# GpSimd's elementwise steps cut into pieces of about 128 columns, in a fused attention, FFT and feed-forward kernel

## The chip, the cores and the metric

The kernel runs on one core of a Trainium2 chip. The metric is the time of one execution on the device in microseconds (us), the median of the runs; less is better.

## What is computed

Inputs are q, k, v of 8 batches x 8 heads x 576 positions x 64, and two weight matrices. All are float32, but the weights, which come as 64-bit floats.

```python
def _attn_ref(q, k, v):
    scores = scale * np.matmul(q, k.transpose(0, 1, 3, 2))
    mask = (rel >= 0) & (rel < 64)
    ...
    return np.matmul(attn, v).astype(np.float32)

def _moe_ref(x, w_ch1, w_ch2):
    X = np.fft.fft(np.fft.fft(x, axis=1), axis=2)
    u = x + np.real(X).astype(np.float32)
    un = (u - mean(u)) / np.sqrt(var(u) + 1e-06)
    return u + np.maximum(un @ w_ch1, 0.0) @ w_ch2
```

So it is attention in a window of 64 positions, a two-dimensional FFT of its result (576 positions by 512 features) of which the real part is added, a normalisation and a feed-forward layer of 512 to 2048 to 512.

## The kernel before

The 8 x 576 = 4608 rows are cut into 36 tiles T of 128 rows; each pair of batches has 9 tiles. The work has four kinds of stages.

`attn_tile(T)` computes attention for a tile. From tile 13 on (`PRO`) operands are split into two float16 parts, a high one (a cast, on ACT or DVE) and a low one, the difference between the float32 value and the high part. The low part is one elementwise subtraction on POOL or DVE: `k_lo` (line 484, 512 columns, from `kn`), `q_part(1)` (line 495, 1024 columns, from `qn`) and `p_lo` (line 620, 512 columns, from `pr`, twice a tile). The parts lie in the buffer `flex` and are turned by transposing DMAs that SP sends: `kst` (line 487), `qbd` (line 499) and `pt` (line 626). TensorE (PE) then computes scores `psc` (line 575) and the product `pa` (line 657). VectorE (DVE) applies the mask (line 587) and scales to `xu` (line 669). `radix4` (line 691) makes five sums `y` of the tile's columns: four instructions, the first two of 256 columns, the last two of 128. The high and low part `yp` of `y` (lines 405 and 758) are turned too, and `keep` (line 718) adds the turned parts into `yT`.

`fft(b)` folds `yT` and makes sums of 388 columns (lines 804 to 858), which PE multiplies by constant matrices (`pg`, `pz`, lines 890 and 924). The result goes to DRAM (`md`).

`norm_tile(T)` gathers rows of `md` (line 998, a DMA that POOL issues), adds them to `xu`, takes mean and variance, the reciprocal root `rs` on POOL (line 1022) and the scaled `un` on DVE (line 1026). Its low part `up` is `u_lo` (line 1045, 512 columns, on POOL or DVE), and a DMA turns it to `uhl`.

`ffn(c)` multiplies two tiles at a time by the weights: `ph` (line 1207), the parts `hh` (ACT, line 1222, and DVE, line 1225), `po` (line 1188), and the last sum into `xu` (line 1245). Its matmuls fill PE wherever the other stages leave room.

The order is made by `Plan.order()` while the program is built. Each step is an `op` with an engine, a duration in us, a priority and often a second engine (`alt`); the planner walks through time with these durations and fixes the engine of each step and the order on each engine. It takes POOL and the DVE steps that are marked `port` to exclude each other. The chip then runs each engine's list in that order, with semaphores between the engines. A step's function is called with the engine that was chosen (`eng`), and issues its instructions there.

Of the kernel before, what the change touches and what calls it, by code (L numbers as in the profile page):

```python
# [19 lines left out]
ALU = mybir.AluOpType  # L20
# [277 lines left out]
def attn_fft_ffn_kernel(ctx: ExitStack, tc: tile.TileContext, q, k, v, w1, w2, gidx, dft_d, dft_s, mask, out):  # L298
    nc = tc.nc
# [14 lines left out]
    op = plan.op  # L314
# [86 lines left out]
    def copy(eng, out, in_, scale=None):  # L401
# [4 lines left out]
        else:  # L406
            eng.tensor_copy(out, in_)

    xts, Bx, yTs, ByT, ByL, uhls, Bu, mds, Bmd = ({} for _ in range(9))

    def attn_tile(T, base):
        pb, n = divmod(T, NT)
# [4 lines left out]
        t = {}  # L417
# [39 lines left out]
        if whole:  # L457
            bpk, bpq = Buf("ps"), Buf("ps")

            def flip(dst, src):  # L460
                t[dst] = bank("ps", f"{dst}{T}")
                for hp in range(4):
                    heads = t[src][:, 2 * hp : 2 * hp + 2].rearrange("p h d -> p (h d)")
                    nc.tensor.transpose(t[dst][:, hp], heads, ident)

            def q_copy(h, eng):
                src = t["pq"][64 * h : 64 * h + 64].rearrange("p a (j s) -> p a j s", j=2)
                copy(eng, qbd32[i][64 * h : 64 * h + 64, :, :, h, :], src)

            op("PE", 0.44, base, lambda: flip("pk", "kn"), [bk, Bid], [bpk, bkT])  # L470
            op("ACT", 0.48, base + 0.1, lambda e: copy(e, kst_, t["pk"]), [bpk], [bkT], alt=("DVE", 0.6), port=False)
            op("PE", 0.44, base + 0.5, lambda: flip("pq", "qn"), [bq, Bid], [bpq, Bq[i]])
            for h in range(2):
                op("ACT", 0.48, base + 0.6, lambda e, h=h: q_copy(h, e), [bpq], [Bq[i]], alt=("DVE", 0.6), port=False)
        else:
            bkp = Bfl[0]

            def k_hi(eng):
                t["kp"] = half[:, 0].rearrange("p (h z d) -> p h z d", h=H, z=2)
                copy(eng, t["kp"][:, :, 0], t["kn"])  # L480

            def k_lo(eng):
                kp = t["kp"]
                eng.tensor_tensor(out=kp[:, :, 1], in0=t["kn"], in1=kp[:, :, 0], op=ALU.subtract)  # L484

            def k_turn():
                nc.sync.dma_start_transpose(kst_, t["kp"].rearrange("p h z d -> p (h z d)"))

            def q_part(z, eng):
                hi, lo = qpad[:, :, 0::3], qpad[:, :, 1:3]  # L490
                src = t["qn"][:, :, None, :].to_broadcast([P, H, 2, D])
                if z == 0:
                    copy(eng, hi, src)
                else:
                    eng.tensor_tensor(out=lo, in0=src, in1=hi, op=ALU.subtract)  # L495

            def q_turn(j):
                src = qpad[64 * j : 64 * j + 64].rearrange("p h x d -> p (h x d)")
                nc.sync.dma_start_transpose(qbd[i][:, j].rearrange("p h (z s) -> p (h z) s", z=2), src)  # L499

            op("ACT", 0.52, base, k_hi, [bk], [bkp], alt=("DVE", 0.34, lazy))
            op("POOL", 1.12, base + 0.1, k_lo, [bk], [bkp], alt=("DVE", 0.6, lazy))
            op("DMA", TURN, base + 0.2, k_turn, [bkp], [bkT], lat=2.0)
            op("ACT", 0.95, base + 0.5, lambda e: q_part(0, e), [bq], Bfl[4:6], alt=("DVE", 0.6, lazy))
            op("POOL", 2.1, base + 0.6, lambda e: q_part(1, e), [bq], Bfl[4:6], alt=("DVE", 1.13, lazy))
            for j in range(2):
                op("DMA", TURN, base + 0.7, lambda j=j: q_turn(j), Bfl[4:6], [Bq[i]], lat=2.8)
# [49 lines left out]
        for jj in range(2):  # L557
            J = 2 * n + jj
            m = ((192 if jj else 128) if J % 9 == 0 else (64 if jj else 0))
# [57 lines left out]

            def p_lo(eng, jj=jj):
                pp = t["pp", jj]
                eng.tensor_tensor(out=pp[:, :, 1], in0=t["pr", jj], in1=pp[:, :, 0], op=ALU.subtract)  # L620

            def p_turn(h, jj=jj):
                if h == 0:
# [58 lines left out]
        def radix4(eng):  # L682
            y = t["y"] = sb([P, 5, P], F32, "y", f"y{T}")
            x4 = xts[T].rearrange("p (a e) -> p a e", a=4)
            for o, p0, p1, al in (
                (y[:, 0::4], x4[:, 0:2], x4[:, 2:4], ALU.add),
                (y[:, 2:4], x4[:, 0:2], x4[:, 2:4], ALU.subtract),
                (y[:, 1], y[:, 0], y[:, 4], ALU.subtract),
                (y[:, 0], y[:, 0], y[:, 4], ALU.add),
            ):  # L690
                eng.tensor_tensor(out=o, in0=p0, in1=p1, op=al)  # L691

        op("POOL", 2.35, base + 7, radix4, [bx], [by], alt=("DVE", 1.2, LAZY_Y if T < 4 else lazy))
        first, keeps = [], []
        for bb in range(2):
# [11 lines left out]
            def keep(eng, bb=bb, b=b, lo=lo, hi=hi):  # L707
                if n == 0 and not soon:
                    yTs[b] = sb([P, 4, S + 1], F32, "yT", f"yT{b}")
                spans = [(lo - S * bb, lo - P * n, hi - lo)]  # L710
                if n == 0:
                    spans.append((S, 0, 1))
                for d_, o, m in spans:
                    dst, src = yTs[b][:, :, d_ : d_ + m], t["py"][..., o : o + m]
                    if soon:
                        copy(eng, dst, src, YS)
                    else:
                        eng.tensor_tensor(out=dst, in0=src[:, 0], in1=src[:, 1], op=ALU.add)

            if lo == S * bb and n > 0:  # L720

# [67 lines left out]
    def fft(b, base):  # L789
        pb, bb = divmod(b, 2)  # L790
        lazy = LAZY_FFT if b else plan.MARGIN
        t = {}
# [5 lines left out]
        def fold(which, c0, c1, eng):  # L798
            yT = yTs[b]
            fw, bw = yT[:, :, c0:c1], yT[:, :, S - c0 : S - c1 : -1]  # L800
            if which == 0:
                if "xe" not in t:
                    t["xe"], t["xo"] = sb([P, 4, HS + 1], F32, "xe", f"xe{b}"), yT[:, :, 0 : HS + 1]
                eng.tensor_tensor(out=t["xe"][:, :, c0:c1], in0=fw, in1=bw, op=ALU.add)
            else:
                eng.tensor_tensor(out=fw, in0=fw, in1=bw, op=ALU.subtract)

        if bb == 0:
            low.append((ByL[b], Buf()))
# [8 lines left out]
        for x, (nm, src, bsrc, o_sum, o_dif) in enumerate((("f", "xe", 1, 0, 2), ("h", "xo", 0, 2, 0))):  # L818
# [3 lines left out]
            def view(src):  # L822
                s_ = t[src]
                return s_[:, :, 0:NJ], s_[:, :, 192 : 192 + NJ], s_[:, :, 192 : 192 - NJ : -1]


            def first(eng, which, al, nm=nm, src=src):
                a0, up, dn = view(src)
                t[nm, which] = sb([P, 4, NJ], F32, "r3", f"{nm}{which}_{b}")
                eng.tensor_tensor(out=t[nm, which], in0=up, in1=dn, op=al)  # L830

            def mid(nm=nm, src=src):
                t[nm, 1] = sb([P, 4, NJ], F32, "r3", f"{nm}1_{b}")
# [2 lines left out]
                )  # L836

            def tot(eng, nm=nm, src=src):
                eng.tensor_tensor(out=t[nm, 0], in0=t[nm, 0], in1=view(src)[0], op=ALU.add)

            pr = base + 1 + x
            two = {"alt": ("POOL", 0.95, lazy)}
# [4 lines left out]
            for r in (2, 1, 0):  # L847
# [7 lines left out]

                def rest(eng, r=r, nm=nm):
                    s_ = t[nm, r, "v"]
                    eng.tensor_tensor(out=s_[:, 1], in0=t[nm, r], in1=s_[:, 0], op=ALU.subtract)

                op("ACT", 0.42, pr + 0.1, part, [b3[r]], [bfh[nm, r]], alt=("DVE", 0.27))  # L860
                op("DVE", 0.47, pr + 0.2, rest, [b3[r]], [bfh[nm, r]], **two)
# [124 lines left out]
    def norm_tile(T, base):  # L986
# [55 lines left out]
            copy(eng, t["up"][:, 0], t["un"])  # L1042

        def u_lo(eng):
            eng.tensor_tensor(out=t["up"][:, 1], in0=t["un"], in1=t["up"][:, 0], op=ALU.subtract)  # L1045

        def u_turn():
            new_u()
# [269 lines left out]
```

## Time and profile before

| | us |
|---|---|
| median of 3 runs | 1019.76 |
| the runs | 1015.79, 1019.76, 1021.48 |
| the profiled execution, first to last instruction | 1015.3 |
| PE busy in it | 972.7 (96%) |
| DVE busy | 679.6 (67%) |
| ACT busy | 417.9 (41%) |
| POOL busy | 197.4 (19%), 203 instructions |

The profiled execution is one of its own; its span, 1015.3 us, is all of its time that the profile shows. [...] An engine's busy time counts an instruction from its start to its end, waits for a shared resource within it too. In brackets behind a row of the timeline stands how long the engine was idle before it and what ended that.

### The profile page before, as it was taken

Reading aid. Unit: us, or ns where it says so; the run is one execution under the profiler, and the core shown is the slowest. Engines: PE = TensorE matmul, PEld = TensorE weight load, DVE = VectorE, ACT = ScalarE, POOL = GpSimd, SP = SyncE. Lnnn points to the kernel's source line nnn. Section 1 sums busy time; section 2 is a strip of 40 time slices with the busy share of each in tenths; the row PEclk is TensorE's granted clock in tenths of the full one; section 3 lists DMA queues with packets and bytes.
Section 4 is the critical chain, followed back from the end, with each engine's and each line's share of the span. In section 5 each row is a group of like instructions: output and inputs, shape, how many; then the busy total and the mean of one; then the engine's idle time right before and its main releaser. Section 6 shows DMA issues by size and latency. Waiting matters only on the chain.

```text
span 1015.3 us, 22449 instructions
## 1 busy us (share of the span) xinstructions
PE 972.7 (96%) x8756; PEld 687.3 (68%) x8756; DVE 679.6 (67%) x1979; ACT 417.9 (41%) x1047; POOL 197.4 (19%) x203
## 2 busy tenths in 40 slices
PE   8889989999999989998999999999999999999998
PEld 7677757676676657665676666766676667676665
DVE  5899899888777767565787769676686636441121
ACT  6666656744554335323354335333453213121111
POOL 1000100042244223332022302233021300220000
PEclk9999999999999999999999999999999999999999
DMA  8987673235989866878668766867565421230000
GB/s 194 244 224 198 191 188 109 71 78 94 160 152 178 160 114 143 142 137 141 126 111 172 144 126 108 173 131 161 89 111 108 94 38 37 60 74 21 1 22 21
DMA packets 310538, 123.06 MB, mean 121 GB/s; under 512 B 292568, under 2 KB 292696, under 8 KB 310432
## 3 DMA queue, kind: packets, MB, share of 16 engines
q1 hardware_dynamic: 307712, 112.71, 54.8%
q0 software_dynamic: 2720, 8.92, 3.3%
q8 instruction: 69, 1.13, 0.5%
q14 instruction: 37, 0.30, 0.1%
HBM read 54.97 MB, written 14.17 MB: 68 GB/s over the span
## 4 chain that ended last, share of the span: by engine, by line
PE 75%; DVE 8%; DMA 8%; SPq 5%; ACT 2%; issue 2%; POOL 0%; DVEq 0%; ACTq 0%; POOLq 0%
PE ph L1207 30%; PE po L1188 30%; PE pz L924 3%; PE pa L657 3%; DMA pt<-flex 2%; DMA kn<-in_k 2%; PE pg L890 2%; PE psc L568 2%; PE psc L575 2%; SPq L626 2%; SPq L499 1%; DVE y L691 1%; PE pp L606 1%; SPq L427 1%; DVE pr L587 1%
## 5 line engine op out<-in xcount | busy, mean ns | idle before, releaser
L1207 PE MATMUL ph<-uhl,w0s 128*128 128x256 f16 (+1 forms) x3384 | 427.1, 277 | 10.1 <-DVE hh L1225 10.1
L1188 PE MATMUL po<-w1s,hh 128*128 128x512 f16 (+1 forms) x1696 | 428.1, 389 | 0.0
L1207 PEld LDWEIGHTS <-w0s 128*128 128x128 f16 x3264 | 318.0, 98 | 97.6 <-issue 14.5
L1225 DVE SCALAR_TENSOR_TENSOR hh<-ph,hh 128x256 f16<-128x256 f32 x272 | 114.5, 422 | 231.7 <-ACT hh L1222 225.8
L1222 ACT ACTIVATE hh<-ph 128x256 f16<-128x256 f32 x272 | 103.6, 382 | 392.9 <-PE ph L1207 297.1
L1188 PEld LDWEIGHTS <-hh 128*128 128x128 f16 x1632 | 157.0, 98 | 138.8 <-issue 1.9
L595 ACT ACTIVATE pr<-pr,nm 128x128 f32<-128x128 f32 x288 | 90.9, 392 | 13.2 <-DVE nm L587 13.1
L587 DVE CUSTOM_DVE_ANT_0 pr<-psc,mskb 128x128 f32<-128x128 f32 x288 | 65.5, 285 | 15.3 <-PE psc L568 11.3
L1045 POOL TENSOR_TENSOR up<-un,up 128x512 f16<-128x512 f32 x33 | 39.7, 1204 | 75.8 <-ACT up L403 73.1
L620 POOL TENSOR_TENSOR flex<-pr,flex 128x512 f16<-128x512 f32 x23 | 27.4, 1190 | 133.8 <-ACT flex L403 93.5
L1022 POOL TENSOR_TENSOR rs<-mv,mhalf 128x1 f32<-128x1 f32 x36 | 21.0, 584 | 157.9 <-DVE mv L1018 152.2
L484 POOL TENSOR_TENSOR flex<-kn,flex 128x512 f16<-128x512 f32 x19 | 25.0, 1314 | 125.0 <-ACT flex L403 119.3
L998 POOL DMA_INDIRECT mt<-md,gix x34 | 36.5, 1073 | 57.4 <-DMA md<-mp 48.8
L657 PE MATMUL pa<-va,pt 128*64 128x65 f16 (+1 forms) x760 | 39.3, 205 | 7.5 <-DMA pt<-flex 7.5
L657 PE MATMUL pa<-ve,pt 128*64 128x65 f16 (+1 forms) x760 | 39.4, 205 | 0.3 <-DMA ve<-va 0.3
L403 ACT CAST flex<-pr 128x512 f16<-128x512 f32 x39 | 24.0, 615 | 23.5 <-DMA pt<-flex 21.1
L691 DVE TENSOR_TENSOR y<-xu 128x256 f32<-128x256 f32 x68 | 32.1, 512 | 0.6
L669 DVE TENSOR_TENSOR xu<-pa,rc 128x256 f32<-128x256 f32 x72 | 30.6, 425 | 2.6
L568 PE MATMUL psc<-kst,qbd 128*128 128x128 f32 x208 | 28.2, 282 | 3.1 <-ACT qbd L403 1.2
L924 PE MATMUL pz<-g,ds__75 97*96 97x257 f16 (+3 forms) x240 | 29.3, 273 | 1.4 <-DVE g L900 1.4
L657 PEld LDWEIGHTS <-pt 128*64 128x64 f16 x1104 | 20.7, 113 | 14.7 <-DMA pt<-flex 7.9
L495 POOL TENSOR_TENSOR flex<-qn,flex 128x1024 f16<-128x1024 f32 x12 | 26.2, 2187 | 16.3 <-ACT flex L403 14.1
(155 smaller groups left out, 1108.0 us busy)
## 6 DMA issues: line engine op xcount, KB each, us to landing
wd<-in_moe_w_ch SPq DMA_DIRECT2D x20, 512.0 KB
out<-xu SPq DMA_DIRECT2D x36, 256.0 KB
ve<-va SPq DMA_DIRECT2D x67, 130.0 KB
kn<-in_k SPq DMA_DIRECT2D x32, 256.0 KB
qn<-in_q SPq DMA_DIRECT2D x32, 256.0 KB
flex<-in_moe_w_ch SPq DMA_DIRECT2D x12, 512.0 KB
flex<-in_v SPq DMA_DIRECT2D x20, 256.0 KB
md<-mp SPq DMA_DIRECT2D x24, 192.0 KB
```

The lines of the kernel that those rows point to most:

```text
L568: nc.tensor.matmul(p_[:, hp], qw, keys(hp, jj), start=True, stop=True)
L587: nc.vector.tensor_tensor_reduce(out=t["pr", jj][:, hp], in0=t["ps", jj][:, hp], in1=mskb[:, m : m + P], scale=-0.125, scalar=3.0e38, op0= ...
L595: nc.scalar.activation(pr, pr, AF.Exp, bias=t["nm", jj][:, hp : hp + 1], scale=-1.0)
L657: nc.tensor.matmul(pa[64 * jj : 64 * jj + 64, hh], pt[:, sl], v_, start=(x == 0), stop=(x == len(mm) - 1))
L691: eng.tensor_tensor(out=o, in0=p0, in1=p1, op=al)
L924: nc.tensor.matmul(pz[:M, c0:c1], ds_[:NJ, a, c[0] : c[0] + c[1]], t["g", gi][:, b_, c0:c1], start=(x == 0), stop=(x == len(mm) - 1),)
L998: nc.gpsimd.indirect_dma_start(out=mts[T], out_offset=None, in_=mds[pb][0 : HR if n < 4 else 2 * HR], in_offset=bass.IndirectOffsetOnAxis( ...
L1045: eng.tensor_tensor(out=t["up"][:, 1], in0=t["un"], in1=t["up"][:, 0], op=ALU.subtract)
L1188: nc.tensor.matmul(t["po"][i], l_, r_, start=(f == 0 and x == 0), stop=(f == NKF - 1 and x == len(mm) - 1))
L1207: nc.tensor.matmul(ph, l_, r_, start=(x == 0), stop=(x == len(mm) - 1))
L1222: nc.scalar.activation(t["hh", f][:, 0], ph, AF.Relu)
L1225: nc.vector.scalar_tensor_tensor(out=hh[:, 1], in0=ph, scalar=0.0, in1=hh[:, 0], op0=ALU.max, op1=ALU.subtract)
```

## The change

A helper `both` takes the place of single elementwise instructions with two inputs. If the engine is POOL it cuts the step along the second dimension into `n` pieces, each an instruction of its own; on DVE it stays one instruction. The planner's durations and priorities are the same, and so are the order on all engines and the choice of the engine for each step.

```diff
+    def both(eng, out, in0, in1, al, n=4):
+        w = out.shape[1] // n if eng is nc.gpsimd else out.shape[1]
+        for k in range(0, out.shape[1], w):
+            eng.tensor_tensor(out=out[:, k : k + w], in0=in0[:, k : k + w], in1=in1[:, k : k + w], op=al)
...
             def k_lo(eng):
                 kp = t["kp"]
-                eng.tensor_tensor(out=kp[:, :, 1], in0=t["kn"], in1=kp[:, :, 0], op=ALU.subtract)
+                both(eng, kp[:, :, 1], t["kn"], kp[:, :, 0], ALU.subtract)
...
                 else:
-                    eng.tensor_tensor(out=lo, in0=src, in1=hi, op=ALU.subtract)
+                    both(eng, lo, src, hi, ALU.subtract, 8)
...
             def p_lo(eng, jj=jj):
                 pp = t["pp", jj]
-                eng.tensor_tensor(out=pp[:, :, 1], in0=t["pr", jj], in1=pp[:, :, 0], op=ALU.subtract)
+                both(eng, pp[:, :, 1], t["pr", jj], pp[:, :, 0], ALU.subtract)
...
-                (y[:, 1], y[:, 0], y[:, 4], ALU.subtract),
-                (y[:, 0], y[:, 0], y[:, 4], ALU.add),
+                (y[:, 1:2], y[:, 0:1], y[:, 4:5], ALU.subtract),
+                (y[:, 0:1], y[:, 0:1], y[:, 4:5], ALU.add),
             ):
-                eng.tensor_tensor(out=o, in0=p0, in1=p1, op=al)
+                both(eng, o, p0, p1, al, o.shape[1])
...
-                        eng.tensor_tensor(out=dst, in0=src[:, 0], in1=src[:, 1], op=ALU.add)
+                        both(eng, dst, src[:, 0], src[:, 1], ALU.add, 4 if m > 1 else 1)
...
         def u_lo(eng):
-            eng.tensor_tensor(out=t["up"][:, 1], in0=t["un"], in1=t["up"][:, 0], op=ALU.subtract)
+            both(eng, t["up"][:, 1], t["un"], t["up"][:, 0], ALU.subtract)
```

The same edit is made in the FFT's folds and sums (lines 804 to 858), of which POOL has two steps of 388 columns, cut in four.

On POOL, where the normalisation of tiles 6 to 8 meets the first split queries (`qn`), the list of instructions before was:

```order
L998 DMA mt_2773<-md_993,gix 128x512
L1045 TENSOR_TENSOR up_2796<-un_2793,up_2796 128x512
L495 TENSOR_TENSOR flex<-qn_1913,flex 128x8x128
L1022 TENSOR_TENSOR rs_2902<-mv_2880,mhalf 128x1
L998 DMA mt_2914<-md_993,gix 128x512
```

On POOL in the same place it is with the change (line numbers are 6 higher, and the helper's line 413 stands for each cut step):

```order
L1004 DMA mt_2788<-md_993,gix 128x512
L413 TENSOR_TENSOR up_2811<-un_2808,up_2811 128x128 x4
L413 TENSOR_TENSOR flex<-qn_1919,flex 128x128 x8
L1028 TENSOR_TENSOR rs_2927<-mv_2905,mhalf 128x1
L1004 DMA mt_2939<-md_993,gix 128x512
```

Nothing has moved: a step is four or eight instructions in its old place, and the same holds along POOL's whole list. On PE, DVE, ACT and SP the lists are alike but for line numbers.

## Rows read from the trace of the kernel before

**Rows 1.** The page: busy time by engine (us, share, instructions), and the chain that ended last.

```profile
PE 972.7 (96%) x8756; PEld 687.3 (68%) x8756; DVE 679.6 (67%) x1979; ACT 417.9 (41%) x1047; POOL 197.4 (19%) x203
...
PE 75%; DVE 8%; DMA 8%; SPq 5%; ACT 2%; issue 2%; POOL 0%; DVEq 0%; ACTq 0%; POOLq 0%
```

**Rows 2.** Timeline of PE: start and duration (us), instruction [idle before, releaser].

```profile
229.44 0.66 PE L750 MATMUL py<-ident,y 128*128 128x128 f32 x4 [1.08 <-DVE y L691]
...
247.70 1.34 PE L575 MATMUL psc<-kst,qbd 128*64 128x128 f16 x32
...
270.33 0.63 PE L750 MATMUL py<-ident,y 128*128 128x128 f32 x4 [0.83 <-DVE y L691]
...
365.85 0.26 PE L657 MATMUL pa<-va,pt 128*64 128x65 f16 x1 [3.76 <-DMA pt<-flex]
...
442.17 0.60 PE L1207 MATMUL ph<-uhl,w0s 128*128 128x256 f16 x4 [0.74 <-DVE hh L1225]
...
466.76 0.49 PE L1207 MATMUL ph<-uhl,w0s 128*128 128x256 f16 x3 [2.79 <-DVE hh L1225]
```

**Rows 3.** Timeline of DVE, delayed and undisturbed steps; x2 are two instructions in a row.

```profile
225.22 1.71 DVE L691 TENSOR_TENSOR y<-xu 128x256 f32<-128x256 f32 x2
226.85 2.53 DVE L691 TENSOR_TENSOR y<-y 128x128 f32<-128x128 f32 x2
...
267.23 2.42 DVE L691 TENSOR_TENSOR y<-xu 128x256 f32<-128x256 f32 x2
269.58 0.60 DVE L691 TENSOR_TENSOR y<-y 128x128 f32<-128x128 f32 x2
...
347.22 2.50 DVE L758 SCALAR_TENSOR_TENSOR yp<-y,yp 128x512 f16<-128x512 f32 x1
...
438.31 2.16 DVE L758 SCALAR_TENSOR_TENSOR yp<-y,yp 128x512 f16<-128x512 f32 x1
...
459.22 2.10 DVE L620 TENSOR_TENSOR flex<-pr,flex 128x512 f16<-128x512 f32 x1 [0.67 <-ACT flex L403]
...
464.74 1.11 DVE L691 TENSOR_TENSOR y<-xu 128x256 f32<-128x256 f32 x2
...
772.45 0.76 DVE L691 TENSOR_TENSOR y<-xu 128x256 f32<-128x256 f32 x2
...
775.34 0.68 DVE L758 SCALAR_TENSOR_TENSOR yp<-y,yp 128x512 f16<-128x512 f32 x1
```

**Rows 4.** Timeline of POOL in three stretches.

```profile
225.44 1.21 POOL L1045 TENSOR_TENSOR up<-un,up 128x512 f16<-128x512 f32 x1 [0.62 <-ACT up L403]
226.61 2.30 POOL L495 TENSOR_TENSOR flex<-qn,flex 128x1024 f16<-128x1024 f32 x1
...
346.77 2.40 POOL L495 TENSOR_TENSOR flex<-qn,flex 128x1024 f16<-128x1024 f32 x1 [2.20 <-ACT flex L403]
...
454.77 1.15 POOL L1045 TENSOR_TENSOR up<-un,up 128x512 f16<-128x512 f32 x1 [6.92 <-ACT up L403]
455.88 0.56 POOL L1022 TENSOR_TENSOR rs<-mv,mhalf 128x1 f32<-128x1 f32 x1
```

**Rows 5.** POOL's instructions by form: count, busy us, mean ns of one, idle before, releasers.

```profile
L1045 POOL TENSOR_TENSOR up<-un,up 128x512 f16<-128x512 f32 x33 | 39.7, 1204 | 75.8 <-ACT up L403 73.1 <-issue 1.9 <-DVE up L407 0.8
...
L620 POOL TENSOR_TENSOR flex<-pr,flex 128x512 f16<-128x512 f32 x23 | 27.4, 1190 | 133.8 <-ACT flex L403 93.5 <-DVE flex L407 33.0 <-DMA kn<-in_k 6.1
L495 POOL TENSOR_TENSOR flex<-qn,flex 128x1024 f16<-128x1024 f32 x12 | 26.2, 2187 | 16.3 <-ACT flex L403 14.1 <-DVE flex L407 2.2
L484 POOL TENSOR_TENSOR flex<-kn,flex 128x512 f16<-128x512 f32 x19 | 25.0, 1314 | 125.0 <-ACT flex L403 119.3 <-DVE flex L407 5.5
...
L691 POOL TENSOR_TENSOR y<-y 128x128 f32<-128x128 f32 x4 | 1.8, 454 | 0.2
```

**Rows 6.** Timeline of SP's queue: first and last of eight rows in a stretch.

```profile
349.75 1.25 SPq L765 DMA_TRANSPOSE py<-yp  x1
...
361.25 1.32 SPq L626 DMA_TRANSPOSE pt<-flex  x1
```

More of the change, by code (lines that the diff above doesn't have):

```diff
@@ L803, in fold @@
                     t["xe"], t["xo"] = sb([P, 4, HS + 1], F32, "xe", f"xe{b}"), yT[:, :, 0 : HS + 1]
-                eng.tensor_tensor(out=t["xe"][:, :, c0:c1], in0=fw, in1=bw, op=ALU.add)
+                both(eng, t["xe"][:, :, c0:c1], fw, bw, ALU.add)
             else:
-                eng.tensor_tensor(out=fw, in0=fw, in1=bw, op=ALU.subtract)
+                both(eng, fw, fw, bw, ALU.subtract)
         if bb == 0:
@@ L829, in first @@
                 t[nm, which] = sb([P, 4, NJ], F32, "r3", f"{nm}{which}_{b}")
-                eng.tensor_tensor(out=t[nm, which], in0=up, in1=dn, op=al)
+                both(eng, t[nm, which], up, dn, al)
             def mid(nm=nm, src=src):
@@ L838, in tot @@
             def tot(eng, nm=nm, src=src):
-                eng.tensor_tensor(out=t[nm, 0], in0=t[nm, 0], in1=view(src)[0], op=ALU.add)
+                both(eng, t[nm, 0], t[nm, 0], view(src)[0], ALU.add)
             pr = base + 1 + x
@@ L857, in rest @@
                     s_ = t[nm, r, "v"]
-                    eng.tensor_tensor(out=s_[:, 1], in0=t[nm, r], in1=s_[:, 0], op=ALU.subtract)
+                    both(eng, s_[:, 1], t[nm, r], s_[:, 0], ALU.subtract)
                 op("ACT", 0.42, pr + 0.1, part, [b3[r]], [bfh[nm, r]], alt=("DVE", 0.27))
```

## The prediction

> **What bounds the kernel now.** I read the page first [rows 1]: TensorE (PE) is busy for 972.7 of 1015.3 us, and the chain of work that ended last spends 75% of its time on PE, 8% on VectorE (DVE), 8% on DMAs, 5% on SyncE's queue and 0% on GpSimd (POOL). So a change on POOL can only pay through a place where PE idles, and only if POOL stands behind that idle time by way of another engine. The reader is to see two things in these rows: that PE's idle time is only some 40 us in all, and that POOL, with 197.4 us of work, is far from being a limit itself.
>
> Then the timeline of PE, to find where it idles for what [rows 2]. After the first 200 us the long gaps are few. Five of them end with a DVE step or with a transposing DMA: 1.08 us at 229.44 (waits for `y`), 0.83 at 270.33 (`y`), 3.76 at 365.85 (`pt`), 0.74 at 442.17 and 2.79 at 466.76 (`hh`).
>
> Then the timeline of DVE just ahead of these gaps [rows 3], read against durations of the same step where nothing is beside it: the pair `y<-y` takes 0.60 us, the pair `y<-xu` 0.76, the step `yp` 0.68. At 226.85 the pair took 2.53, at 267.23 the pair `y<-xu` took 2.42, at 347.22 `yp` took 2.50, at 438.31 2.16. Beside the first and the third, POOL's timeline [rows 4] has a 1024-column step: 226.61 to 228.91, and 346.77 to 349.17. DVE's step ends about 0.5 us behind POOL's. So a DVE step that reads two operands from SBUF stands still while POOL reads SBUF, and goes on when POOL's instruction is over. The five gaps together are 9.2 us, which is about the whole stake: what else DVE loses beside POOL is time that PE never waits for.
>
> What happens when two POOL instructions stand back to back is in the same rows: `up` ends at 226.65 and the 1024-column step begins at 226.61, and yet the second `y<-xu` was over at 225.22 + 1.71 = 226.93, in the middle of the 1024-column step. DVE came in at the seam, for one instruction, and the next `y` then waited for the whole following POOL step. The two engines take turns, instruction by instruction. This is what the change acts on.
>
> **The change, part by part.** PE, DVE, ACT and SP keep their rows; nothing is moved past anything. On POOL, 75 steps of 512 columns become four pieces and 12 steps of 1024 columns become eight [rows 5], which is 75 x 3 + 12 x 7 = 309 more instructions; the five `yT` steps, two steps of 388 columns and two radix steps bring it to 334. The later pieces wait for nothing but older POOL work.
>
> Price of a piece. From 512 to 1024 columns POOL needs 2187 - 1204 = 983 ns more, 1.92 ns a column; so 1204 - 983 = 221 ns are fixed. A piece of 128 columns is then 246 + 221 = 467 ns, and the only step of 128 columns in the trace has 454 [rows 5]. A step of 512 columns goes from 1.20 to about 1.82 us (+0.62), one of 1024 from 2.19 to 3.63 (+1.45), and POOL has about 334 x 0.21 = 70 us more to do, some 267 us in 1015. As instructions overlap a little at the seams (0.04 us at 226.6), 0.17 a piece is the low end; 0.23 the high one. [...]
>
> What covers these 0.6 to 1.45 us. The first 1024-column step ends at 228.91, its transposes are sent right behind, and PE reads the result at 247.70 [rows 2, 4]: 19 us, against a step that ends 1.45 us later, or 3 us later with DVE's turns in between. That is the typical case for keys, queries and probabilities. The `up` steps feed a feed-forward chunk, which PE takes up only when it has nothing else to do. With that cover gone, each would cost its 0.6 to 1.45 us in full. One thing is queued on POOL with no cover: at 455.88 the reciprocal root `rs` starts the moment the `up` step from 454.77 is over [rows 4], and DVE waits for `rs`; it would come 0.6 us later. I count that in the last term below.
>
> The sum, place by place; after the change a DVE step waits for at most one piece, 0.45 us, each time it reads two operands:
> - 229.44: four `y` steps took 4.2 us (225.22 to 229.4) where they need 0.76 + 0.60 = 1.4 undisturbed. With three waits of a piece it is 2.7, so 1.5 less, more than the gap: -1.1.
> - 270.33: 2.42 - 0.76 = 1.66 us of waits, all in the first pair; the four `y` can now wait four times 0.45 = 1.8 while POOL goes on in pieces. Between 0 and -0.8; I take -0.2, as the waits nearly cancel.
> - 365.85: `yp` at 347.22 waited 2.50 - 0.68 = 1.82, now 0.45, so its transpose leaves 1.37 earlier than 349.75. From there SP sends eight rows without a real pause up to the `pt` transpose at 361.25 [rows 6] on which this gap ends. Against that, what came ahead of `yp` on POOL is 0.6 later. Between 0 and -1.4; I take -0.7, the middle.
> - 442.17: `yp` at 438.31 waited 1.48, the gap is 0.74: -0.7 (between 0 and -0.74).
> - 466.76: the step at 459.22 took 2.10 and needs about 0.69 (estimated as one 512-column step with two operands, like `yp`), so it gains 0.96; the four `y` at 464.74 waited 1.11 - 0.76 = 0.35 for a key step and may now wait up to 1.4. Between +0.5 and -1.8; I take -0.5.
> - All other places: shorter gaps ahead of which a DVE step waited (some 2 us of gap), against `rs` that is 0.6 later and new turns with `y`. I take 0, with -2 and +3 as ends.
>
> Together -3.2 us against the profiled execution's 1015.3 us, so 1012.1 us of span. That execution lies by the lowest of the three runs, 1015.79, and 4.5 below their median of 1019.76. The same 3.2 off the median gives **1016.6 us**. A measurement of this kernel can tell about 0.5%, 5.1 us, from no change, so this forecast counts as no difference. Its own range is 1013.5 to 1019.5.
>
> **The rivals.**
> 1. The waits go altogether, and PE gets all of it: 1.1 + 0.8 + 1.4 + 0.7 + 1.8 = 5.8 us, and 2 more from the short gaps, so 1012 to 1014. For it: all five gaps have a POOL step in their history, and one turn of DVE at the seam shows. Against it: a run of four `y` steps meets four pieces, where now it meets one step.
> 2. It becomes slower, by the turns. While POOL has a piece left, every two-operand DVE step waits for one. A run of four such steps beside a 512-column step waits up to 4 x 0.45 = 1.8, where it waited up to 1.2 once: 0.6 more, on some 80 steps, so 48 us more on DVE. As the chain has DVE on it for 8% of the span while DVE is busy for 67% [rows 1], about one eighth reaches the end: +6 us, 1025.8. It decides from the point where DVE's runs of two-operand steps beside POOL are on average longer than two. Against it: of the six delayed rows in [rows 3] three are single steps (347.22, 438.31, 459.22), and only `y` comes in runs.
> 3. The pieces don't let DVE in. Then a DVE step waits 0.6 to 1.45 longer in each of the five places, 3 to 6 us together with what lies between, 1023 to 1026. [...] The row at 225.22, where DVE came in at a seam of two overlapping steps, speaks against it.
> 4. It reaches nothing: DVE gets shorter, and PE's gaps stay since other transfers end there just as late. 1019 to 1021. For it: the 3.76 us gap ends with a DMA, and the rows between are SP's.
>
> **How the numbers follow.** Forecast 0.47, rival 1 0.22, rival 2 0.12, rival 3 0.05, rival 4 0.14. Rival 1 is mostly faster by over 0.5% (below 1014.7), as is a small part of the forecast's range: 0.25. Rival 2 and part of rival 3 are slower by over 0.5% (above 1024.9): 0.14. The rest, 0.61, is within. The range leaves out most of rival 2 and the far end of rival 1: 1011.5 to 1023.5.
>
> **What would show it.** POOL's busy time at 255 to 270 us and the pieces at 0.42 to 0.47 us each; the two `yp` steps at 1.2 or less and the 1024-column waits of over 1.5 us gone from DVE; DVE's busy time, 679.6 now, 3 to 15 us lower; the gaps of the first and the fourth place gone, and the third at 2.3 to 3.4. Wrong it would be if DVE's busy time rose, if new gaps of PE ended with `y` or `hh` behind runs of two-operand steps, or if POOL showed on the chain of waits.

## The result, and the profile after

The changed kernel takes 1010.51 us (median of 10 runs, 1003.20 to 1014.95) where the kernel before takes 1019.94 (10 runs, 1015.79 to 1023.75): a ratio of 0.9906, 95% interval 0.9877 to 0.9936. A second comparison later gave 0.9903 (0.9878 to 0.9927). So it is some 9.5 us faster. The prediction was 1016.6, with 1011.5 to 1023.5 as its range: right in sign, too small by a factor of three, and just outside the range.

The profiled execution of the changed kernel took 1003.44 us, 7 us below the median of its runs. A run's time is 1.7 to 1.9 us more than its span here, so that of before (span 1015.3) took some 1017, about 3 below its median. The two traces are therefore 13.8 us apart where the medians are 9.4 apart: they show more than a typical pair of runs would. The page of the changed kernel, busy time and chain, against [rows 1]:

```profile
span 1001.5 us, 22810 instructions
PE 967.4 (97%) x8756; PEld 685.3 (68%) x8756; DVE 665.6 (66%) x1979; ACT 418.2 (42%) x1047; POOL 260.9 (26%) x537
PE 80%; DMA 8%; SPq 3%; DVE 3%; issue 2%; ACT 2%; POOL 1%; DVEq 0%; POOLq 0%; ACTq 0%
```

The first thing to see is that PE's idle time, span less busy time, went from 42.6 to 34.1 us, and that PE's busy time went down as well, by 5.3 us with the same 8756 matmuls. DVE's share of the chain fell from 8% to 3%. POOL's busy time rose by 63.5 us, as the pieces cost what was forecast. POOL by form, against [rows 5] (count, busy us, mean ns of one, idle before it with the releasers):

```profile
L413 POOL TENSOR_TENSOR up<-un,up 128x128 f16<-128x128 f32 x132 | 56.0, 452 | 64.8 <-ACT up L403 62.2 <-issue 1.6 <-DVE up L407 0.8
L413 POOL TENSOR_TENSOR flex<-qn,flex 128x128 f16<-128x128 f32 x96 | 44.5, 496 | 14.1 <-ACT flex L403 10.9 <-DVE flex L407 3.2
```

PE's timeline, the gaps that answer to [rows 2] and one that is new:

```profile
309.09 0.22 PE L663 MATMUL pa<-va,pt 128*64 128x65 f16 x1 [2.10 <-DMA pt<-flex]
...
362.30 0.22 PE L663 MATMUL pa<-va,pt 128*64 128x65 f16 x1 [1.43 <-DMA pt<-flex]
...
459.29 1.47 PE L1213 MATMUL ph<-uhl,w0s 128*128 128x256 f16 x12 [1.30 <-DVE hh L1231]
```

The 3.76 us gap at `pt` is down to 1.43, the 2.79 at `hh` to 1.30; those of 1.08 (`y`), 0.83 (`y`) and 0.74 (`hh`) are gone. The 2.10 us at 309.09 are new. So is a gap that ends with `y`, one of the signs of being wrong that the prediction named; it is small:

```profile
367.26 0.63 PE L756 MATMUL py<-ident,y 128*128 128x128 f32 x4 [0.82 <-DVE y L413]
```

DVE's and POOL's timelines ahead of the `pt` gap show why; they answer to the row at 347.22 of [rows 3] and 346.77 of [rows 4]:

```profile
341.88 0.94 DVE L413 TENSOR_TENSOR y<-y 128x128 f32<-128x128 f32 x2
...
343.50 0.93 DVE L536 SCALAR_TENSOR_TENSOR va<-flex,va 128x512 f16<-128x512 f32 x1 [0.35 <-ACT va L534]
...
345.58 0.64 DVE L405 TENSOR_SCALAR yp<-y 128x512 f16<-128x512 f32 x1 [0.81 <-DVE hh L1231]
346.25 0.80 DVE L764 SCALAR_TENSOR_TENSOR yp<-y,yp 128x512 f16<-128x512 f32 x1
```
```profile
345.51 3.75 POOL L413 TENSOR_TENSOR flex<-qn,flex 128x128 f16<-128x128 f32 x8 [1.63 <-ACT flex L403]
```

`yp` takes 0.80 us where it took 2.50 and is over at 347.05, while the POOL step beside it goes on until 349.26. DVE comes in between pieces.

The fall of PE's busy time is in part the clock. Stretches behind the two long gaps, of the kernel before and then of the changed one (length; busy time of PE, its weight loads, DVE, ACT and POOL; the granted TensorE clock as a share; DMA share; GB/s):

```profile
365.00:370.00 5.00, 4.15 (x55) 2.71 (x56) 4.33 (x12) 1.25 (x2) 3.18 (x2) 0.66 0.33 53
...
460.00:470.00 10.00, 7.21 (x40) 4.19 (x40) 8.42 (x33) 4.93 (x13) 3.13 (x3) 0.89 1.00 153
470.00:480.00 10.00, 10.00 (x68) 6.66 (x67) 3.60 (x7) 2.08 (x4) 0.49 (x1) 0.94 0.76 153
```
```profile
365.00:370.00 5.00, 4.18 (x43) 2.96 (x42) 4.93 (x16) 2.14 (x6) 1.64 (x4) 1.00 0.70 121
...
460.00:470.00 10.00, 10.00 (x70) 6.66 (x69) 4.46 (x8) 2.46 (x5) 0.12 (x1) 1.00 1.01 202
470.00:480.00 10.00, 10.00 (x137) 6.90 (x136) 4.94 (x21) 3.85 (x10) 1.78 (x5) 1.00 0.48 74
```

Behind a gap of 3.76 us PE runs part of the next 5 us at a granted clock of 0.50 (366 to 368 of before): a mean of 0.66, so 5 x 0.34 = 1.7 us of work lost. Behind the gap of 2.79 us it is 10 x 0.11 + 10 x 0.06 = 1.7 again. In this trace of the changed kernel both stretches stand at 1.00. So 3.4 of the 5.3 us are clock that did not fall in these two places; the other 1.9 are not traced. My sum had no such term. It is not a sure gain: in a second trace of the changed kernel (`again`) both places stand at 1.00 too, but the clock fell behind the new gap at 309, which was 1.95 us long there, and the mean over the whole span was 0.993, as in before (0.996 in the first trace). The stretch behind that gap, from `again` and then from the first trace, where the gap was 2.10:

```profile
310.00:313.00 3.00, 3.00 (x33) 2.25 (x30) 1.40 (x6) 0.73 (x2) 2.08 (x5) 0.50 1.29 262
```
```profile
310.00:313.00 3.00, 3.00 (x23) 2.12 (x22) 2.28 (x8) 1.28 (x3) 1.44 (x4) 1.00 1.26 286
```

### The profile page after: what moved, and what is told of

Same layout as the page of the kernel before. It is cut to its first block, busy times and chain, and to the rows that moved or that the text cites. A ratio compares the mean times of both kernels' runs of the same rounds, so it can differ in the third digit from the quotient of the medians.

```text
span 1001.5 us, 22810 instructions
## 1 busy us (share of the span) xinstructions
PE 967.4 (97%) x8756; PEld 685.3 (68%) x8756; DVE 665.6 (66%) x1979; ACT 418.2 (42%) x1047; POOL 260.9 (26%) x537
## 3 DMA queue, kind: packets, MB, share of 16 engines
q8 instruction: 69, 1.13, 0.5%
## 4 chain that ended last, share of the span: by engine, by line
PE 80%; DMA 8%; SPq 3%; DVE 3%; issue 2%; ACT 2%; POOL 1%; DVEq 0%; POOLq 0%; ACTq 0%
PE ph L1213 34%; PE po L1194 32%; DMA kn<-in_k 3%; PE pa L663 3%; PE pz L930 2%; PE psc L581 2%; PE pg L896 2%; DMA pt<-flex 2%; PE psc L574 2%; POOL flex L413 1%; SPq L632 1%; DMA kst<-flex 1%; PE pp L612 1%; SPq L505 1%; DMA qn<-in_q 1%
## 5 line engine op out<-in xcount | busy, mean ns | idle before, releaser
L413 POOL TENSOR_TENSOR up<-un,up 128x128 f16<-128x128 f32 x132 | 56.0, 452 | 64.8 <-ACT up L403 62.2
L413 POOL TENSOR_TENSOR flex<-kn,flex 128x128 f16<-128x128 f32 x76 | 40.4, 561 | 111.9 <-ACT flex L403 85.3
L413 POOL TENSOR_TENSOR flex<-pr,flex 128x128 f16<-128x128 f32 x92 | 38.7, 451 | 117.4 <-ACT flex L403 88.6
L413 POOL TENSOR_TENSOR flex<-qn,flex 128x128 f16<-128x128 f32 x96 | 44.5, 496 | 14.1 <-ACT flex L403 10.9
L574 PEld LDWEIGHTS psc<-kst,qbd 128*128 128x128 f32 x208 | 25.1, 192 | 6.2 <-ACT pt L403 2.3
```

What stands on the lines that cost most here:

```text
L413: eng.tensor_tensor(out=out[:, k : k + w], in0=in0[:, k : k + w], in1=in1[:, k : k + w], op=al)
L574: nc.tensor.matmul(p_[:, hp], qw, keys(hp, jj), start=True, stop=True)
```

## The experiments

The expectations weigh these theories. A: the gain is the sum of many waits, each now as long as a piece reads. B: a wait lasts a whole piece. C: the gain comes from POOL's results being later. D (called rival D): too many pieces cost more than they bring. E: the 1024-column steps carry it. F: one place, the seventh 1024-column step (at 346.77), carries it. F2: the gain outside the seventh lies in the other named places of the sum. F3: it lies in places that the sum put at nothing. G and H come with the last group. All kernels are the changed one with an edit in `both`, unless said otherwise.

| run | what is cut | ratio to before (95%) | POOL busy, us | gap at `pt`, us | key load lands after, us |
|---|---|---|---|---|---|
| the change | all, 128 columns | 0.9906 (0.9877-0.9936) | 260.9 | 1.43 | 4.07 |
| p256 | all, 256 columns | 0.9919 (0.9889-0.9948) | 220.0 | 0.38 | 3.91 |
| p64 | up and keys 64, rest 128 | 0.9986 (0.9965-1.0006) | 303.9 | 3.47 | 5.14 |
| q_only | the twelve, in eight | 0.9925 (0.9898-0.9952) | 212.2 | 0.50 | 4.05 |
| q4 | the twelve, in four | 0.9915 (0.9883-0.9946) | 203.0 | 0.68 | 3.82 |
| q_whole | all but the twelve | 0.9973 (0.9953-0.9993) | 247.1 | 3.59 | 5.31 |
| late | none, results late | 1.0065 (1.0043-1.0087) | 281.7 | 3.69 | 4.98 |
| q7 | the seventh | 0.9956 (0.9939-0.9972) | 198.8 | 1.09 | 3.96 |
| q_not7 | the other eleven | 0.9956 (0.9933-0.9979) | 212.1 | 4.43 | 5.87 |

"The twelve" are the 1024-column steps; "lands" is from the row of SP that issues the key load `kn` just ahead of that gap to the DVE step that reads it (360.06 and 365.47 in the trace of before: 5.41).

**How large a piece.** p256 puts `n = max(1, n // 2)` at the head of `both`, p64 `n = 2 * n if out.shape[1] % (2 * n) == 0 else n`. In p64 the 1024-column and the probability steps cannot be cut further on that axis and stay at 128 columns, so its text says too much there.

> The change with half as many pieces: 256 columns each (the four yT, up, key and probability steps in two pieces, the 1024-column steps in four). Price of a piece 221 + 256 x 1.92 = 712 ns. Theory A (a DVE step waits only while a piece reads, 1.92 ns a column, and comes in during the fixed 0.2 us): waits of about 0.49 us, POOL busy 222 to 228 us, the two yp steps near 1.2, nearly all of the gain kept: 1011 to 1014. Theory B (a DVE step waits for a whole piece): waits of 0.7 us each, the four y steps at 1.5 to 2.2, gaps of 0.5 to 1 us back in front of py: 1014 to 1018. Theory C (the gain comes from POOL's results being later, and so from another order of meeting of the transfers): a third of the lengthening, a third of the gain: 1016 to 1018, or a jump either way.

> The change with twice as many pieces: 64 columns each where the step can be cut so (up, keys, probabilities in eight, the 1024-column steps in sixteen; yT and y stay at 128). Price of a piece 221 + 64 x 1.92 = 344 ns, so POOL goes from 261 to about 345 us. Theory A: waits of 0.12 us each, which is no gain beside 0.23, and outputs 0.8 to 1.7 us later: 1009 to 1012, the same as the change. Theory B: waits of 0.34 instead of 0.45: 1008 to 1011. Theory C: the gain grows with POOL's lengthening, by more than as much again: 1000 or less, or a jump. Rival D (more turns cost DVE more, and POOL comes into the chain): DVE busy above 670 us and 1013 to 1018.

p256 keeps the gain (1008.21 us, where the kernel before took 1016.76 beside it); p64 loses it (1014.79). The longest waits follow theory A. One DVE step beside pieces of each width, from p64 (beside 64-column keys), p256 (beside 256-column queries) and before (the pair beside a 512-column key step):

```profile
344.60 0.81 DVE L537 SCALAR_TENSOR_TENSOR va<-flex,va 128x512 f16<-128x512 f32 x1 [0.63 <-ACT va L535]
```
```profile
455.95 1.20 DVE L414 TENSOR_TENSOR flex<-pr,flex 128x512 f16<-128x512 f32 x1 [0.73 <-ACT flex L403]
```
```profile
343.14 1.58 DVE L691 TENSOR_TENSOR y<-y 128x128 f32<-128x128 f32 x2
```

Undisturbed these take 0.69, 0.69 and 0.60, so they waited 0.12, 0.51 and 0.98; beside 128 columns `va` at 343.50 (above) waited 0.24, and beside 1024 a cast that began with the POOL step waited 1.97 (2.40 instead of 0.43, shown under `late`; `yp` of [rows 3] came 0.45 us into the step and waited 1.82). That is about 1.9 ns a column, the part of a POOL step that grows with its columns, without its 0.2 us of fixed cost. A step that comes in the middle of a piece waits less (0.08 to 0.24 beside 128 columns in the trace of the change). What p64 shows against all of A to C is that the shortest waits bring the least gain. Its key step lasts 2.61 us (1.16 in before, 1.68 in the change), and the profile puts the idle time of DVE's cast ahead of `yp` down to it (1.56 us, about 0.8 in the other two):

```profile
344.03 2.61 POOL L414 TENSOR_TENSOR flex<-kn,flex 128x64 f16<-128x64 f32 x8
```
```profile
347.31 0.43 DVE L405 TENSOR_SCALAR yp<-y 128x512 f16<-128x512 f32 x1 [1.56 <-POOL flex L414]
```

The `pt` gap is back at 3.47. Pieces that are too fine pay at the very place where coarse ones did; rival D holds, by another way than DVE's busy time (it expected over 670 us; 662.6 is the lowest of all).

**Which steps.** q_only: `n = n if n == 8 else 1`; q_whole: `n = 1 if n == 8 else n`; q4: `n = 4 if n == 8 else 1`.

> Only the twelve 1024-column steps are cut, in eight; all others stay whole as before. Theory A: the waits at 226.85 and 347.22 go (places 1 and 3 of the sum, with the stretch at a lower granted clock behind the 3.76 us gap), the others stay with 0.9 us each: about half of the gain, 1013 to 1016; POOL busy 212 to 216 us. Theory E (it is the 1024-column steps alone): all of the gain, 1009 to 1012. Theory C: 84 of 334 added instructions, a quarter of the gain: 1017 to 1018.

> All steps are cut as in the change, only the twelve 1024-column steps stay whole. Theory A: the waits of 1.7 to 1.9 us behind 1024 columns are back, with the 3.76 us gap at pt and the lower clock behind it; about half of the gain: 1013 to 1017; POOL busy 243 to 247 us. Theory E: nothing of the gain is left, 1019 to 1021. Theory C: three quarters of the gain: 1012 to 1013.

> The twelve 1024-column steps in four pieces of 256 columns, all others whole. Wait per turn 0.49 us, step 2.85 instead of 3.6 us, POOL busy 201 to 206 us. Theory F and theory A: the yp step at 1.2 or less, the gap at pt under 1.5, 1007 to 1010, the same as with eight pieces. If the finer cut matters: 1011 to 1014.

q_only has 1008.17 beside 1016.76, q4 1008.22 beside 1018.53: the twelve steps alone, with 84 or 36 added instructions instead of 334, bring what the change brings, as far as can be measured. With the 1024-column steps whole and all others cut (q_whole, 1014.91) 0.27% is gained, 0.07 to 0.47. Theory E would leave nothing there, so it holds nearly, not fully.

**Whether lateness is the gain.** No step is cut; the last column is computed again, so that the step's result is late by as many instructions as the change adds:

```
        eng.tensor_tensor(out=out, in0=in0, in1=in1, op=al)
        if eng is nc.gpsimd and in0 is not out:
            e = (slice(None), *(slice(d - 1, d) for d in out.shape[1:]))
            for _ in range(1, n):
                eng.tensor_tensor(out=out[e], in0=in0[e], in1=in1[e], op=al)
```

> No step is cut; each step that the change cuts does its whole width and then repeats its last column as often as the change adds pieces (3 or 7 times), so that its result comes as late as with pieces or later, and POOL has the 70 us more or some 100, but DVE still waits for the whole step. Theory C (the gain comes from POOL's later results): 1006 to 1011. Theories A and F: nothing gained, and the lateness by itself costs what the cuts of the smaller steps lost: 1017 to 1024, DVE's waits of 1.8 us as before.

1025.63 beside 1018.53, a little more than A and F allowed: POOL's lengthening by itself (84 us here, 63.5 in the change) costs 0.65%. Theory C falls, and so does the zero that the prediction put on it. This trace also shows that not only steps with two SBUF operands wait for POOL: the cast ahead of `yp` takes 2.40 beside the whole 1024-column step, 0.43 otherwise. Why a cast, which reads one, waits too is not shown.

```profile
352.30 2.40 DVE L405 TENSOR_SCALAR yp<-y 128x512 f16<-128x512 f32 x1 [1.10 <-POOL flex L415]
```

**Which of the twelve.** A counter in `both` numbers the 1024-column steps on GpSimd; the others and all smaller steps stay whole. The edit of q7, where the set in the condition is (2 to 6, 8 to 12 and 1) in q_not7, (1, 3, 9, 10) in q_named, (2, 4, 5, 6, 8, 11, 12) in q_rest, and (1, 3, 7, 9, 10) with four pieces in q_five:

```
        if eng is nc.gpsimd and n == 8:
            seen.append(1)
        n = 8 if n == 8 and len(seen) == 7 else 1
```

> Before's whole steps, and of the twelve 1024-column steps only the seventh (at 346.77 us in the trace of before, beside the yp step that waited 1.82 us) cut in eight. Theory F (one place carries the gain: yp, its transpose, the pt transpose behind it, the 3.76 us gap and the stretch at 0.66 of the clock that follows): the gap down to 1.5 or less and 1010 to 1013. Theory A (the gain is the sum of many waits): a fifth of it, 1015 to 1016. Theory C (later results): 7 of 334 instructions, no change: 1016 to 1017.

> Eleven of the twelve 1024-column steps cut in eight, the seventh whole, and all others whole. Theory F: the 3.5 us gap at pt stays with the low clock behind it, and 1014 to 1017. Theory A: four fifths of the gain, 1009 to 1011. Theory C: as with all twelve, 1008 to 1010.

> Before's whole steps, and of the 1024-column steps only the first, third, ninth and tenth cut in eight: the four named places of the sum other than the seventh (229.44, 270.33, 442.17, 466.76). Theory F2 (the gain outside the seventh lies in the named places): the gaps at 229 and 442 gone, the one at 467 at 2.3 or less, 1014 to 1016 with before at 1018.5. Theory F3 (it lies in places that the sum put at nothing): no more than 1 us of gain, 1017 to 1019.

> The other seven of the twelve (second, fourth, fifth, sixth, eighth, eleventh, twelfth) cut in eight, all else whole. Theory F2: 1017.5 to 1019.5 with before at 1018.5. Theory F3: 1014 to 1016.

> Only the five 1024-column steps of the five places of the sum (first, third, seventh, ninth, tenth) cut, in four pieces of 256 columns; 15 added instructions instead of 334, POOL busy 199 to 201 us. By the runs so far the seventh is worth 4 to 4.5 us; under F2 the other four 2.5 to 4: 1010 to 1012 with before at 1018.5, as good as the whole change. Under F3: 1013 to 1014.5.

> The changed kernel as it is, on the chip of the three others, to have its ratio beside theirs: 0.988 to 0.994 of before. If it is near 0.992 as with the twelve 1024-column steps alone, the cuts of the smaller steps bring nothing that can be measured.

The seventh alone brings 0.44% (0.28 to 0.61; 4.5 us), its gap falls to 1.09, and the other four of the five gaps of [rows 2] are still there (1.09, 0.59, 0.75 and 2.76). The other eleven bring 0.44% (0.21 to 0.67) with that gap at 4.43. Neither theory is met: F asked for nearly all of the gain from the seventh, A for a fifth. Of the eleven, the four named places bring 0.30% (0.02 to 0.58; 1016.37 beside 1017.71), the other seven 0.31% (0.12 to 0.51; 1013.90). The five together bring 0.43% (0.24 to 0.62; 1013.85), no more than the seventh by itself, so the parts do not simply add up, or the intervals hide it. The change again: 1007.64. So about half of the gain is one place; the other half is spread, in places that the sum named and in places that it put at nothing.

One such place comes and goes without a cut step beside it. In the trace of before PE also idles 2.28 us at 783.33; the step `hh` that ends this stands on DVE behind `yT`, and `yT` waits for the transpose `py` (rows of PE, then of POOL, SP and DVE):

```profile
783.33 1.47 PE L1207 MATMUL ph<-uhl,w0s 128*128 128x256 f16 x12 [2.28 <-DVE hh L1225]
```
```profile
775.42 1.51 POOL L998 DMA_INDIRECT mt<-md,gix  x1 [6.12 <-DMA md<-mp]
776.09 1.24 SPq L765 DMA_TRANSPOSE py<-yp  x1
782.25 0.69 DVE L718 TENSOR_TENSOR yT<-py 128x512 f32<-128x512 f16 x1 [3.62 <-DMA py<-yp]
```

In the changed kernel the gap is gone, and the same three rows are:

```profile
763.79 1.03 POOL L1004 DMA_INDIRECT mt<-md,gix  x1 [5.63 <-DMA md<-mp]
764.58 1.24 SPq L771 DMA_TRANSPOSE py<-yp  x1
768.49 0.69 DVE L413 TENSOR_TENSOR yT<-py 128x512 f32<-128x512 f16 x1 [1.42 <-DMA py<-yp]
```

The step `yp` ahead of it was undisturbed in before [rows 3, 775.34]. What differs is how early POOL's gather `mt` starts before the transpose: where it leads by 0.70 us or less `yT` starts 5.76 to 6.17 us after the transpose's issue (ten of the eighteen traces), where it leads by 0.79 or more 3.65 to 3.92 (eight). The long form is in before, p256, p64, q_whole, late, q_named, q_five, b_less, a_more and a_less, the short one in the change, `again`, q_only, q4, q7, q_rest, q_not7 and b_more; q7 and b_more have no pieces anywhere near. That two transfers meet there is argued from these rows alone, as no run changes it by itself. But 2.2 of the 13.8 us between the two traces lie here and not in a shorter wait of DVE beside POOL, and so do 2.3 of the 3.5 us by which the trace of q_rest is shorter than that of before. It is also a difference between q7 and q_five, which gained alike.

In q_not7 it was the cast and not `yp` that stood beside the whole step (2.27 us), and the gap came all the same: what counts is when the pair is done.

**Why the gap fell by 2.3 us where `yp` came 1.7 sooner.** The table's last column falls in two groups: with a long gap the key load lands 5.0 to 5.9 us after its issue, with a short one 3.8 to 4.1, and the `pt` transpose behind it 4.1 to 5.0 or 3.0 to 3.6. The DMA view tells the groups apart. It gives packets, MB and the time of the packets as a share of the time of the core's 16 DMA engines, here for 361.5 to 364 us of before and then for 359.1 to 361.1 of the change, both while the key load is in flight:

```profile
q1 hardware_dynamic: 1665, 0.41, 126.0%
q8 instruction: 1, 0.02, 2.7%
```
```profile
q1 hardware_dynamic: 1558, 0.38, 95.6%
```

By these rows a packet took 30 ns on average in before and 20 in the change. Queue 8 carries instructions: 69 loads, 1.13 MB in the whole run, 16 KB each, about one for every 254 of PE's 17512 matmuls and weight loads. That they are PE's code is shown by the shifts below; their number is the same with 334 more instructions on POOL. In before one of them starts 3.16 us after the key load's issue and takes 1.07 us; the last packets then trickle, at 5 to 12 GB/s, until 365.2. In the change it starts at 361.15, as the key load's last 0.3 us go. By the DMA records of all runs in the table, such a load began 1.8 to 3.2 us after the key load's issue where the gap is long, and 3.5 us or later where it is short. Theory G: it is the cause. Rival H: it only stands beside it. The test leaves GpSimd and VectorE alone and shifts PE's code by 32 instructions: b_less is the kernel before with 16 of the 80 warm-up matmuls left out, b_more with 16 narrow ones more; a_less and a_more are the changed kernel with the same edits.

```
                for _ in range(add):
                    nc.tensor.matmul(warm[:, 0:64], wide[:, 0:P], wide[:, 0:64], start=True, stop=True)
                add = 0
```

> The kernel before, with 16 of TensorE's 80 warm-up matmuls at the start left out, so that every later place in TensorE's code lies 32 instructions nearer to the page's start and a page's load is asked for 32 instructions later. Theory G (the 16-KB load of TensorE's next code page, at 363.22 us in the trace of before, falls into the key load's burst and makes it land 1.3 us later): the code load comes after the gap, the key load lands 3.8 to 4.1 us after its issue instead of 5.4, the pt transpose 3.0 to 3.6 instead of 4.6, and that gap is 2.0 to 2.7 instead of 3.76, with yp still waiting 1.8. Rival H (what is late is the transposes themselves, the code load only beside them by chance): 5.0 or more and a gap of 3.5 or more as before. Whole time: 2 to 3 us less under G if the other pages' shifts even out, which nothing excludes from going either way.

> The kernel before, with 16 narrow warm-up matmuls (64 columns) more at the start: code loads are asked for 32 instructions earlier. Theory G: the code load comes some 0.5 to 1 us earlier, still between the key load's issue and its burst's end, so the key load still lands 5 us or more after its issue and the gap stays at 3.4 or more. Rival H: the same; so this one tells only whether any shift of the code changes the gap. Whole time as before within 3 us.

> The changed kernel with 16 narrow warm-up matmuls more. Theory G: the code load that came 3.5 us after the issue of the key load comes 0.5 to 1 us earlier and into the burst: the key load lands after 5 us or more, and the gap grows from 0.9 to 1.4 to 2.2 to 2.8, with yp as quick as in the change; 1 to 3 us of the gain are lost. Rival H: 3.9 to 4.1, a gap of 0.9 to 1.5.

> The changed kernel with 16 warm-up matmuls left out. Theories G and H: the code load comes later still, the key load lands 3.8 to 4.1 us after its issue and the gap stays at 0.9 to 1.5; whole time as the change within 3 us, 0.988 to 0.994 of before.

b_less, rows of SP, DVE and PE: the instruction load has gone to 5.44 us after the key load's issue, the key load lands after 3.98, the transpose after 3.08, and the gap is 2.63, although `yp` still takes 2.50:

```profile
364.60 1.21 SPq L427 DMA_DIRECT2D kn<-in_k  x1
365.85 1.32 SPq L626 DMA_TRANSPOSE pt<-flex  x1
...
368.58 0.43 DVE L407 CAST flex<-kn 128x512 f16<-128x512 f32 x1 [3.32 <-DMA kn<-in_k]
...
368.93 0.22 PE L657 MATMUL pa<-va,pt 128*64 128x65 f16 x1 [2.63 <-DMA pt<-flex]
```

a_more, the changed kernel with the load put back (1.75 us after the issue), although `yp` takes 0.80:

```profile
358.07 1.09 SPq L433 DMA_DIRECT2D kn<-in_k  x1
359.20 1.99 SPq L632 DMA_TRANSPOSE pt<-flex  x1
...
362.93 0.43 DVE L407 CAST flex<-kn 128x512 f16<-128x512 f32 x1 [2.29 <-DMA kn<-in_k]
...
363.30 0.22 PE L663 MATMUL pa<-va,pt 128*64 128x65 f16 x1 [1.61 <-DMA pt<-flex]
```

The key load lands after 4.86 and the transpose after 4.10: a little under what G said (5), far from H (3.9 to 4.1). The gap is only 1.61 and not the 2.2 to 2.8 expected. In b_more, with the load 0.87 us after the issue, the key load lands after 4.76, but the gap is 2.72 where both theories said 3.4 or more. So G is shown for the landing, by shifts both ways, and not for the length of the gap. That also depends on when PE gets there, which the rows tell (start of the row at `pt`, less its gap, less the issue of the key load): 2.0 us after the issue in before, 2.3 in b_more and 1.7 in b_less, but 3.2 in the change and 3.6 in a_more, where `yp` is sooner and SP with it. a_less (landing 3.96, gap 2.60) has 1.7 although `yp` took 0.80; its trace is of the slowest of its ten runs (1020.45). q_rest is an exception that I cannot explain: key load 4.04, transpose 4.77, gap 2.98.

The whole time did not follow that one place. b_less: 1020.10 beside 1016.15, a ratio of 1.0015 (0.9985 to 1.0045), where 2 to 3 us less were hoped for; b_more: 1024.62, 1.0085 (1.0057 to 1.0114), outside the 3 us that I gave it; a_more 1013.48, 0.9976 (0.9956 to 0.9997); a_less 1010.71, 0.9938 (0.9914 to 0.9961). All loads shift, and the start changes. But the pairs with equal PE code tell how solid the change is: b_more to a_more 1.1% faster, b_less to a_less 0.8%, before to after 0.9 to 1.0%.

No version beat the changed kernel by more than the measurement tells; q4 and q_only equal it with far fewer instructions.

## Why the prediction was wrong

**Right.** The mechanism, the price and the seam. POOL's busy time is 260.9 (said: 255 to 270), pieces of 128 columns 0.43 to 0.56 us (0.42 to 0.47; those of keys and queries are dearer), DVE's busy time fell by 14.0 (3 to 15). `yp` is below 1.2, the first and fourth gaps are gone. The rival by which the pieces don't let DVE in is refuted by the row of `va` at 343.50 and by DVE's busy time; so is the slower rival of turns in the form given, since DVE's busy time fell, and fell further with finer pieces.

**"A DVE step waits for at most one piece, 0.45 us".** In the trace of the change one such step waits 0.28 at most (`xu` at 680.70 took 0.97 where 0.68 to 0.70 is usual), near the 0.25 that 128 columns take without POOL's fixed 0.2 us; `un` at 319.05, with one full-width operand, took 1.02 where 0.54 is usual. The size of the wait did not decide: p256 waits 0.5 a turn and keeps the gain. Nor is "at most one piece" always so: in p256 a `yp` at 435.29 took 1.96 us, a wait of 1.28 over two seams, and the same `yp` waits as long in q4.

**"365.85: ... I take -0.7, the middle".** This step failed most: the term was put at 0.7 us, and cutting the one POOL step there brought 4.5 (2.9 to 6.2). The transpose `py` did leave about as much earlier as said, but the sum ended there, and the gap, said to end at 2.3 to 3.4, is 1.43 in the change and 1.09 in q7. In the trace of q7 three things make it up. PE comes to the gap 3.2 us after the key load's issue and not 2.0, as SP's rows are that much sooner beside PE's: 1.2 us, where the range ended at 1.4. The data for `pt` is there 4.3 us after that issue and not 5.8, as an instruction load no longer meets the key load: 1.5 us. And the clock stays at 1.00 from 366 to 374: 1.7 us. Together that is 4.4. The second is partly luck, since it hangs on where a 16-KB load of PE's code falls: b_less has it without any piece, and its whole time is no better than before.

**"Five of them end with a DVE step or with a transposing DMA" and "All other places: ... I take 0".** The list of gaps was short. The trace of before has five more of over 1 us behind the first 200, which end with `hh` or `pt`: 1.27 at 379.87, 1.78 at 417.62, 1.28 at 555.73, 1.17 at 572.69 and 2.28 at 783.33, 7.8 us together, so the five chosen ones (9.2) were not the whole stake. In the change they are 0.93, 0.73, 1.25, 1.18 and gone. The seven 1024-column steps outside the five places bring 3.2 us (1.2 to 5.2) when cut alone, where the sum had nothing; in the one trace of that kernel, 3.5 us shorter than that of before, 2.3 are the gap at 783.33, which no cut step stands beside. How much of the 3.2 us is shorter waits and how much is such meetings of transfers stays open.

**"The sum ... 229.44, 270.33, 442.17, 466.76", -2.5 together.** Measured 3.1 (0.2 to 5.9) with these four cut alone: agrees, weakly. The four, the seventh and the other seven come to 10.8 us, more than the twelve together bring (7.6 in q_only, 8.7 in q4), so these terms do not simply add up, or the intervals hide it.

**Cover of the later results, put at nothing.** `late` shows that it is not free: 7 us for 84 us of POOL time. In the change the shorter waits pay for it; in p64 they don't any more.

The range failed for the same reason: rival 1 (all waits gone, 1012 to 1014) was the nearest, and it, too, counted gaps alone and no clock or landing times behind them. The prediction also set the span of the profiled execution (1015.3) beside times of runs (1015.79), which are some 1.8 us more than their spans; nothing hung on it.

## What to carry to other kernels

When a VectorE step stands still beside a GpSimd step, cut the few long GpSimd steps that do it, and leave the short ones whole: twelve steps in four pieces brought what cutting them all brought (ratios of 0.9915 and 0.9906), and cutting the key and `up` steps finer lost it again (0.9986). Price a gap of PE not by its length alone: read the granted clock in the stretch behind it, and ask which other transfer meets the one that ends it. And test a gain of 1% against a small shift of PE's code, as that alone moved this kernel by nearly as much (0.85% in b_more).

## What the runs showed that was not expected

- Instruction loads delayed data here. One 16-KB load of PE's code inside a 256-KB key load made that land 4.8 to 5.9 us after its issue instead of 3.8 to 4.1, in eight of the eighteen traces; shifting the code by 32 instructions took the effect away in one kernel and put it into the other. In whole time, 16 narrow warm-up matmuls made the kernel before 0.85% slower, which shifts all the other loads as well.
- A transpose that was issued 0.70 us or less behind a gather landed 2 us later than one issued 0.79 or more behind it (5.76 to 6.17 us against 3.65 to 3.92, all eighteen traces, one place), and PE idled some 2 us for it.
- A wait of VectorE beside GpSimd was about 1.9 ns for each column of the GpSimd instruction (0.12 us at 64, 0.24 at 128, 0.5 at 256, 0.98 at 512, 1.97 at 1024) where the step comes at its start, not its whole duration, and it also met a cast with one SBUF operand (2.27 and 2.40 us instead of 0.43).
- Repeating one column on GpSimd cost 0.29 us for `up`, 0.38 for keys and 0.33 for queries (three or seven in a row in `late`), where a piece of 128 cost 0.45 to 0.56 in the change: more than half of it is there with one column.
- The clock fell for part of 5 us behind the idle 3.76 us, and again behind 2.79; at 1.43 and 1.30 it stayed at 1.00. Length alone does not tell: in two traces of the changed kernel it fell to 0.50 behind a gap of 1.95 and stayed at 1.00 behind the same gap of 2.10.
